# Transposing x on VectorE and through DRAM instead of on TensorE, in a linear attention with a gated MLP behind it

## The chip, the cores and the metric

One NeuronCore of one Trainium2 chip runs the whole program in one launch. The metric is the device time of an execution in microseconds; of the kernel before there are three runs, and their median counts. The engines' names are those of the profile: PE (TensorE matmuls; PEld is its weight loads), DVE (VectorE), ACT (ScalarE), POOL (GpSimd) and SP (SyncE, which here only issues DMAs).

## The reference

Attention with a feature map, for 4 batches of 4 heads, 1088 tokens and 32 dimensions, followed by a gated MLP with an RMS norm; the 4 x 1088 tokens are 4352 rows of 128:

```
phi(x)  = outer(S1 x, S2 x), 8 x 8 = 64 features per token and head
kv, z   = sum over tokens of phi(k) v, phi(k)
x       = phi(q) kv / (phi(q) z + 1e-6)           # 128 = 4 heads x 32 per token
xn      = x / sqrt(mean(x^2) + 1e-6) * rms_g
out     = (silu(xn @ w_gate) * (xn @ w_val)) @ w_out   # 128 -> 1536 -> 128
```

All inputs are float32; the MLP's weights and S1, S2 reach the chip as 64-bit words and are turned into float32 there.

## The kernel before, in words

**Tiling.** The tokens go in nine chunks, eight of 512 and one of 256. The 1536 hidden units go in 12 blocks of 128 (`j`). A *slot* is one chunk with one block: gate, value and down product (`slot`, L707). Each product is three matmul passes over 512 columns, since every operand is split into a high and a low fp32r part (`w_hi`, `w_lo`, `x_hi`, `x_lo`, `h_hi`, `h_lo`): lines 726 and 764. ACT takes the silu (L735), DVE multiplies (L738), ACT and DVE or POOL split the result (L753, L756).

**Ahead of the slots.** `kside(b)` (L450) makes batch b's kv: a matmul of the keys with `sblk` (S1 and S2 as blocks, L485), outer products (L439), and the sum over tokens on PE (L497; 64 columns of the array at a time for batch 0, 32 for the others). `qside(c)` (L528) makes chunk c's x: features `phiq`, then per 128 tokens the numerators and denominators (`nmm`, L620 to 630: PE holds 64 tokens of phiq as weights, 66 columns of kv stream through, two such tiles stand side by side in the array), the division (L636), the mean of squares (L655), its power on POOL (L668), the scaling `xn` (L671 or L688), a PE transpose of each 128 x 128 piece against an identity (`turn`, L673 to 675), and the split of the result, read from PSUM, into `x_hi` (ACT, L678) and `x_lo` (DVE, L681). From the third chunk on, phiq itself is built from matmul results that are stored to DRAM (`far`, L584) and read back in two layouts (`at`, `bt`, L596 and L602).

**S and the weights.** S is loaded by a DMA of ACT's queue (L392); an ACT and five DVE instructions (L371 to 389) make `sblk` from it, without which no matmul but the warming ones (L337) can start. Each of the 12 weight pieces (384 KB, L412) becomes float32 by five instructions of 128 x 384 (`to_f32`, L341), kept whole in `w_f`.

**What sets the order.** Every instruction is a task of a planner (`Plan`). A table of numbers (`ORDER`, L48) gives the order of all tasks, and a string (`ON`, L86) the engine of those that may run on several. The planner's own costs only place warming matmuls into gaps. So every engine, and SP's queue, runs its list strictly in order. At most eight DMAs of SP are in flight; the ninth waits for the first.

Of the kernel before, what the change touches and what calls it, by code (L numbers as in the profile page):

```python
# [84 lines left out]
"""  # L85
# [9 lines left out]
DEN_ACT = 60  # L95
QHALVES = 1
ABROWS = 1
WRAW = 7
LO_POOL, SCALED_ACT, PUT_ACT, COPY_DVE, PHI_POOL, H_POOL = 600, 100, 0, 300, 400, 900
UNIT, GAP, SPARE = 226, 400, 300  # L100
COLD = 5500
# [767 lines left out]
```

## Time and profile before

| | |
|---|---|
| median of 3 runs | 258.64 us (258.35 to 259.91) |
| profiled execution, span from the first to the last instruction | 256.5 us |
| PE busy | 252.0 us, 98% |
| DVE, ACT, POOL busy | 168.6, 153.8, 90.6 us |
| PE's share of the chain that ended last | 95% |

The page gives the profiled execution by its span alone; the median of the runs is 2.1 us above it, which is what lies around the instructions. Starts are counted from the span's start. A matmul's own duration overlaps the next one's, so the pace of PE is read from the differences of starts. A row with x32 is 32 instructions that follow one another; a float32 matmul stands as two instructions, a float32 transpose as one.

### The profile page before, as it was taken

The page shows a single profiled execution, that of the slowest core. Times are in us where ns is not written, and L with a number is a line of the kernel's source. Part 1 is how long each engine was busy: PE and PEld are TensorE (multiplying, and loading weights), DVE is VectorE, ACT ScalarE, POOL GpSimd, SP SyncE. Part 2 cuts the span into 40 slices and gives each one's busy share as a digit, 9 for nine tenths or more (in the row PEclk, how much of TensorE's full clock was granted, in tenths as well). Part 3 has the DMA queues.
Part 4 walks back from the last instruction along what each step waited for, and adds up shares of the span by engine and source line. Part 5 has one row for each costly group of instructions (what it writes and reads, how often), then busy time and mean ns, then how long its engine had stood idle before and what let it go on. Part 6 is the DMA issues. An engine that isn't in the chain of part 4 may idle for free.

```text
span 256.5 us, 5598 instructions
## 1 busy us (share of the span) xinstructions
PE 252.0 (98%) x2116; PEld 204.0 (80%) x2116; DVE 168.6 (66%) x390; ACT 153.8 (60%) x339; POOL 90.6 (35%) x92
## 2 busy tenths in 40 slices
PE   7999999999999999999999999999999999999995
PEld 5888777788887787788887888888888887888895
DVE  2998999989866676646464666647644554635643
ACT  3789888647664744575555555455556655554572
POOL 3444222123755412583516503145223714132031
PEclk9999999999999999999999999999999999999999
DMA  7999886064015115061320120001000100100010
GB/s 236 380 382 279 251 236 208 0 158 130 1 59 149 65 47 139 0 185 43 92 75 3 42 78 15 0 1 43 0 0 0 41 4 0 41 0 3 0 42 20
DMA packets 13498, 22.13 MB, mean 86 GB/s; under 512 B 1952, under 2 KB 5024, under 8 KB 13472
## 3 DMA queue, kind: packets, MB, share of 16 engines
q1 hardware_dynamic: 13040, 21.52, 27.0%
q8 instruction: 16, 0.26, 0.4%
q10 hardware_dynamic: 432, 0.26, 0.3%
q14 instruction: 10, 0.08, 0.1%
HBM read 18.69 MB, written 3.08 MB: 85 GB/s over the span
## 4 chain that ended last, share of the span: by engine, by line
PE 95%; ACT 2%; DMA 1%; POOL 1%; DVE 0%; issue 0%
PE g_ps L726 28%; PE v_ps L726 28%; PE o_ps L764 28%; PE att L627 3%; PE att L497 2%; PE att L675 2%; DMA s_raw<-sw 1%; PE att L485 1%; PE att L578 1%; PE o_ps L497 1%; ACT phiq L309 0%; ACT w_tmp L362 0%; POOL at L439 0%; PE att L745 0%; PE g_ps L485 0%; PE g_ps L558 0%
## 5 line engine op out<-in xcount | busy, mean ns | idle before, releaser
L738 DVE TENSOR_TENSOR h<-v_ps,s 128x512 f32<-128x512 f32 (+2 forms) x110 | 69.9, 649 | 49.7 <-PE v_ps L726 25.7
L756 POOL TENSOR_TENSOR h_lo<-h,h_hi 128x512 fp32r<-128x512 f32 (+1 forms) x43 | 53.0, 1242 | 109.2 <-DVE h_lo L756 39.7
L735 ACT ACTIVATE s<-g_ps 128x512 f32<-128x512 f32 (+1 forms) x108 | 60.8, 574 | 39.8 <-PE g_ps L726 32.7
L753 ACT CAST h_hi<-h 128x512 fp32r<-128x512 f32 (+1 forms) x106 | 61.3, 599 | 38.6 <-DVE h L738 35.5
L756 DVE TENSOR_TENSOR h_lo<-h,h_hi 128x512 fp32r<-128x512 f32 (+1 forms) x63 | 40.8, 660 | 13.4 <-ACT h_hi L753 10.0
L726 PE MATMUL g_ps<-x_hi,w_hi 128*128 128x512 f32 (+1 forms) x110 | 42.5, 387 | 0.0
L726 PE MATMUL v_ps<-x_hi,w_hi 128*128 128x512 f32 (+1 forms) x110 | 42.3, 385 | 0.0
L726 PE MATMUL g_ps<-x_lo,w_hi 128*128 128x512 f32 (+1 forms) x110 | 41.6, 379 | 0.0
L726 PE MATMUL v_ps<-x_hi,w_lo 128*128 128x512 f32 (+1 forms) x110 | 41.6, 378 | 0.0
L726 PE MATMUL g_ps<-x_hi,w_lo 128*128 128x512 f32 (+1 forms) x110 | 41.5, 378 | 0.0
L726 PE MATMUL v_ps<-x_lo,w_hi 128*128 128x512 f32 (+1 forms) x110 | 41.5, 379 | 0.0
L764 PE MATMUL o_ps<-h_hi,w_hi 128*128 128x512 f32 (+1 forms) x106 | 41.3, 389 | 0.0
L764 PE MATMUL o_ps<-h_hi,w_lo 128*128 128x512 f32 (+1 forms) x106 | 40.7, 384 | 0.0
L764 PE MATMUL o_ps<-h_lo,w_hi 128*128 128x512 f32 (+1 forms) x106 | 40.6, 383 | 0.0
L726 PEld LDWEIGHTS g_ps<-x_hi,w_hi 128*128 128x128 f32 x110 | 20.7, 188 | 4.8 <-ACT s L735 0.2
L726 PEld LDWEIGHTS v_ps<-x_hi,w_hi 128*128 128x128 f32 x110 | 20.7, 188 | 4.6 <-DVE h L738 0.3
L726 PEld LDWEIGHTS g_ps<-x_lo,w_hi 128*128 128x128 f32 x110 | 20.7, 188 | 4.2
L726 PEld LDWEIGHTS v_ps<-x_lo,w_hi 128*128 128x128 f32 x110 | 20.6, 188 | 4.2
L726 PEld LDWEIGHTS v_ps<-x_hi,w_lo 128*128 128x128 f32 x110 | 20.7, 188 | 4.0
L726 PEld LDWEIGHTS g_ps<-x_hi,w_lo 128*128 128x128 f32 x110 | 20.7, 188 | 3.9
L764 PEld LDWEIGHTS o_ps<-h_lo,w_hi 128*128 128x128 f32 x106 | 19.9, 188 | 4.3
L764 PEld LDWEIGHTS o_ps<-h_hi,w_hi 128*128 128x128 f32 x106 | 19.9, 188 | 4.1
(97 smaller groups left out, 256.5 us busy)
## 6 DMA issues: line engine op xcount, KB each, us to landing
w_raw<-w SPq DMA_DIRECT2D x12, 384.0 KB
bt<-far SPq DMA_DIRECT2D x24, 128.0 KB
at<-far SPq DMA_DIRECT2D x12, 256.0 KB
outT<-o_sb SPq DMA_DIRECT2D x8, 256.0 KB
q<-qT SPq DMA_DIRECT2D x7, 256.0 KB
vt<-v SPq DMA_DIRECT2D x4, 272.0 KB
kt<-kT SPq DMA_DIRECT2D x4, 256.0 KB
vt<-v SPq DMA_DIRECT2D x3, 340.0 KB
```

What stands on the lines that cost most here:

```text
L485: nc.tensor.matmul(out=ab()[n0:rows.stop, (t - lo) * HALF:(t - lo + 1) * HALF], lhsT=kt()[:, s0:s0 + len(rows)], rhs=sblk, start=True, sto ...
L497: nc.tensor.matmul(out=kvv[r0:r0 + wide, h // 2, :], lhsT=phi()[:, t, h * F + f:h * F + f + wide], rhs=vt()[:, t, h, :], start=(t == 0 and ...
L578: nc.tensor.matmul(out=accs[p]()[a * D:(a + 1) * D, :m], lhsT=sab[rows, p].rearrange("p c o r -> p (c o r)"), rhs=q()[rows, a * m:(a + 1) ...
L627: nc.tensor.matmul(out=nv[n0:rows.stop, t, p, :], lhsT=phi()[:, p, l0:l0 + len(rows)], rhs=kvs[cut][:, p, :], start=True, stop=True,)
L675: nc.tensor.transpose(out=xt()[:, t * P:(t + 1) * P], in_=xn()[:, t, :], identity=ident)
L726: nc.tensor.matmul(out=acc()[:, cs], lhsT=wt[:, j, i3, :], rhs=x()[:, cs], start=(i == 0), stop=(i == 2))
L735: act(n, lambda: nc.scalar.activation(out=s()[:, :n], in_=gps()[:, :n], func=AF.Silu), cols(gps, whole[0]), [s])
L738: cs.stop - cs.start, lambda cs=cs: nc.vector.tensor_tensor(out=h()[:, cs], in0=vps()[:, cs], in1=s()[:, cs], op=ALU.mult),
L753: act(n, lambda: nc.scalar.copy(out=h_hi()[:, :n], in_=h()[:, :n]), hs, [h_hi], True)
L756: eng.tensor_tensor(out=h_lo()[:, :n], in0=h()[:, :n], in1=h_hi().bitcast(F32)[:, :n], op=ALU.subtract)
L764: nc.tensor.matmul(out=o_ps()[:, :n], lhsT=wt[:, j, 2, :], rhs=x()[:, :n], start=first and i == 0, stop=last and i == 2,)
```

## The change

From the third chunk on (`XT = 2`, `spread`), x is no longer transposed by PE. The scaled x is written into `xn` in the order head, tile, dimension; one DVE instruction transposes each 32 x 32 block of it (`xq`); four DMAs of SP, one per head, store the blocks to DRAM (`turned`) in rows of 128 tokens (512 B each), and one more loads the whole, now with the 128 features on the partitions, to `xt` in SBUF. ACT's and DVE's split into x_hi and x_lo reads `xt` there and not from PSUM. For that layout the numerators are taken with 32 tokens as weights and not 64: twice as many matmuls of the same 66 columns, four tiles side by side. S is loaded by SP's queue and no longer by ACT's. The whole float32 weights live in a rotating buffer (`w_full`, three of them), and only the last two blocks' output weights are copied to `w_f`. `ORDER` and `ON` are new throughout.

```diff
+XT = 2
...
-    plan.add({"dma": Way(
-        ISSUE + SLATE, P * NB * 8 / 320, lambda: nc.scalar.dma_start(out=s_raw.rearrange("p n c -> p (n c)"), in_=sw.bitcast(U32)), since=740
-    )}, (), ["s_raw"])
+    load(P * NB * 8, lambda: nc.sync.dma_start(out=s_raw.rearrange("p n c -> p (n c)"), in_=sw.bitcast(U32)), ["s_raw"])
...
-            def nmm(u=u, num=num):
+            wide = D if spread else HALF
+
+            def nmm(u=u, num=num, wide=wide):
                 nv = num()[:, :4 * 66].rearrange("p (t a x) -> p t a x", t=2, a=2)
                 for t in range(2):
                     for p in range(2):
-                        for rows in range(HALF), range(HALF, P):
-                            l0, n0 = (u + t) * P + rows.start, rows.start
-                            cut = (s0 + l0) // S
+                        for n0 in range(0, P, wide):
+                            l0 = n0 // D * g + (u + t) * D if spread else (u + t) * P + n0
                             nc.tensor.matmul(
-                                out=nv[n0:rows.stop, t, p, :], lhsT=phi()[:, p, l0:l0 + len(rows)], rhs=kvs[cut][:, p, :],
-                                start=True, stop=True,
+                                out=nv[n0:n0 + wide, t, p, :], lhsT=phi()[:, p, l0:l0 + wide], rhs=kvs[(s0 + l0) // S][:, p, :], start=True, stop=True,
                             )
...
+            if spread:
+                xq, xt = sb("xq", [P, 4 * DM], 1), sb("xt", [P, 512], 1)
+                dve(n, lambda: nc.vector.transpose(out=xq()[:, :n], in_=xn()[:, :n]), [(xn, u)], [xq], True)
+                turned = plan.buf(dram, [DM, 512], F32, "turned", 2)
+
+                for h in range(H):
+                    def put_far(h=h, turned=turned, xq=xq):
+                        nc.sync.dma_start(
+                            out=turned()[h * D:(h + 1) * D, :n].rearrange("d (a s) -> a d s", a=4), in_=xq()[:, h * g:(h + 1) * g]
+                        )
+
+                    plan.add({"dma": Way(ISSUE, 200, put_far)}, [xq], [(turned, h)])
+                load(P * n * 4, lambda: nc.sync.dma_start(out=xt()[:, :n], in_=turned()[:, :n]), [xt], [(turned, h) for h in range(H)])
+                got = [xt]
+            else:
+                xt = ps("att", ATT)
...
```

Two places of the new order. First PE around the third chunk's numerators; `phiq` is the weights, `kv` streams. Before:

```order
L726 MATMUL g_ps_1012<-x_hi_571,w_hi 128x512
L726 MATMUL g_ps_1012<-x_hi_571,w_lo 128x512
L726 MATMUL g_ps_1012<-x_lo_589,w_hi 128x512
L627 MATMUL att_1021<-kv_75,phiq_892 64x66 x8
L627 MATMUL att_1036<-kv_73,phiq_892 64x66
L627 MATMUL att_1036<-kv_75,phiq_892 64x66
```

And now:

```order
L761 MATMUL g_ps_911<-x_hi_439,w_hi 128x512
L761 MATMUL g_ps_911<-x_hi_439,w_lo 128x512
L761 MATMUL g_ps_911<-x_lo_460,w_hi 128x512
L638 MATMUL att_921<-kv_75,phiq_879 32x66 x16
L638 MATMUL att_941<-kv_73,phiq_879 32x66
L638 MATMUL att_941<-kv_75,phiq_879 32x66 x3
```

The matmuls are twice as many and half as wide, and they stand earlier, ahead of gate matmuls that still read the first chunk's x. The group `L675 MATMUL att_1259<-ident,xn_1232 128x128 x4` that followed later on PE has no successor.

Second the start of the program on DVE, where `sblk` is made from `s_raw`. Before:

```order
L371 TENSOR_SCALAR s_top<-s_raw 128x64
L382 TENSOR_SCALAR s_tmp<-s_tmp 128x64
L374 SCALAR_TENSOR_TENSOR s_top<-s_raw,s_top 128x64
L386 TENSOR_SCALAR s_tmp<-s_tmp 128x64
L389 TENSOR_TENSOR sblk<-s_tmp,s_top 128x64
L310 COPY both_143<-att_127 128x128
L439 TENSOR_TENSOR at_152<-att_127,both_143 128x512
```

And now:

```order
L346 TENSOR_SCALAR w_tmp_114<-w_raw_100 128x384
L374 TENSOR_SCALAR s_top<-s_raw 128x64
L385 TENSOR_SCALAR s_tmp<-s_raw 128x64
L388 TENSOR_SCALAR s_tmp<-s_tmp 128x64
L352 TENSOR_SCALAR w_tmp_114<-w_tmp_114 128x384
L377 SCALAR_TENSOR_TENSOR s_top<-s_raw,s_top 128x64
L392 TENSOR_SCALAR s_tmp<-s_tmp 128x64
L356 TENSOR_SCALAR w_tmp_114<-w_tmp_114 128x384
L395 TENSOR_TENSOR sblk<-s_tmp,s_top 128x64
L360 SCALAR_TENSOR_TENSOR w_tmp_114<-w_raw_100,w_tmp_114 128x384
L363 SCALAR_TENSOR_TENSOR w_full_145<-w_raw_100,w_tmp_114 128x384
```

The first weight piece's five instructions now stand among those that make `sblk`, and on SP's queue its 384 KB DMA stands first and S's second:

```order
L414 DMA w_raw_100<-w 128x768
L397 DMA s_raw<-sw 128x128
L462 DMA kt_106<-kT 128x512
L529 DMA q_102<-qT 128x256
L462 DMA kt_106<-kT 128x641
```

Before, SP's list began with the three last of these kinds, keys, queries, keys, and S was ACT's.

## Rows read from the trace of the kernel before

**Rows 1.** The page, its head and part 1: busy time, share, instructions.
```profile
span 256.5 us, 5598 instructions
...
PE 252.0 (98%) x2116; PEld 204.0 (80%) x2116; DVE 168.6 (66%) x390; ACT 153.8 (60%) x339; POOL 90.6 (35%) x92
```

**Rows 2.** The page's chain of waits, by engine.
```profile
PE 95%; ACT 2%; DMA 1%; POOL 1%; DVE 0%; issue 0%
```

**Rows 3.** Windows: stretch, busy us of each engine, PEclk, DMA share, GB/s.
```profile
22.21:235.81 213.60, 213.60 (x1621) 170.87 (x1618) 141.25 (x306) 127.95 (x263) 78.41 (x69) 1.00 0.23 68
```

**Rows 4.** PE's timeline around one group of transposes: start, us, engine, line, tiles.
```profile
70.34 0.39 PE L726 MATMUL v_ps<-x_hi,w_lo 128*128 128x512 f32 x1
70.57 0.39 PE L726 MATMUL v_ps<-x_lo,w_hi 128*128 128x512 f32 x1
70.81 0.60 PE L675 MATMUL att<-ident,xn 128*128 128x128 f32 x4
...
71.48 0.39 PE L764 MATMUL o_ps<-h_hi,w_lo 128*128 128x512 f32 x1
```

**Rows 5.** PE's timeline: numerators of one chunk, and of one and a half.
```profile
53.54 1.16 PE L627 MATMUL att<-kv,phiq 128*64 128x66 f32 x32
54.63 0.50 PE L726 MATMUL g_ps<-x_hi,w_hi 128*128 128x512 f32 x1
...
163.85 1.62 PE L627 MATMUL att<-kv,phiq 128*64 128x66 f32 x48
165.40 0.50 PE L726 MATMUL v_ps<-x_hi,w_hi 128*128 128x512 f32 x1
```

**Rows 6.** PE's timeline: a batch's kv, 32 columns of the array each.
```profile
50.26 0.40 PE L726 MATMUL v_ps<-x_lo,w_hi 128*128 128x512 f32 x1
50.59 1.44 PE L497 MATMUL att<-vt,phi 128*32 128x34 f32 x144
51.95 0.50 PE L764 MATMUL o_ps<-h_hi,w_hi 128*128 128x512 f32 x1
52.29 0.39 PE L764 MATMUL o_ps<-h_hi,w_lo 128*128 128x512 f32 x1
```

**Rows 7.** PE's timeline: query matmuls alone, and with a batch's kv behind them.
```profile
26.71 0.40 PE L726 MATMUL g_ps<-x_lo,w_hi 128*128 128x512 f32 x1
...
27.75 0.39 PE L726 MATMUL g_ps<-x_hi,w_lo 128*128 128x512 f32 x1
...
86.23 0.40 PE L764 MATMUL o_ps<-h_lo,w_hi 128*128 128x512 f32 x1
...
88.64 0.39 PE L726 MATMUL g_ps<-x_hi,w_lo 128*128 128x512 f32 x1
```

**Rows 8.** The timeline of the start, all engines; in brackets idle time before.
```profile
0.73 0.41 ACTq L392 DMA_DIRECT2D s_raw<-sw  x1
...
4.01 0.20 DVE L371 TENSOR_SCALAR s_top<-s_raw 128x64 uint32<-128x64 uint32 x1 [3.14 <-DMA s_raw<-sw]
...
5.04 0.34 PE L485 MATMUL g_ps<-sblk,kt 128*64 128x64 f32 x4 [0.70 <-DVE sblk L389]
...
5.99 0.69 DVE L439 TENSOR_TENSOR at<-att,both 128x512 f32<-128x512 f32 x1
6.31 1.07 POOL L439 TENSOR_TENSOR at<-both 128x512 f32<-128x512 f32 x1
...
7.43 0.66 PE L558 MATMUL g_ps<-ident,at 128*128 128x128 f32 x4
```

**Rows 9.** DVE's timeline: instructions that turn a weight piece into float32.
```profile
20.75 0.35 DVE L350 TENSOR_SCALAR w_tmp<-w_tmp 128x384 uint32<-128x384 uint32 x1
21.02 0.35 DVE L346 TENSOR_SCALAR w_tmp<-w_tmp 128x384 f32<-128x384 f32 x1
21.29 0.55 DVE L354 SCALAR_TENSOR_TENSOR w_tmp<-w_raw,w_tmp 128x384 uint32<-128x384 uint32 x1
```

**Rows 10.** SP's timeline: a store to DRAM in four DMAs, and the load behind it.
```profile
146.58 1.74 SPq L584 DMA_DIRECT2D far<-abt  x4
149.54 0.56 SPq L596 DMA_DIRECT2D at<-far  x1
```

**Rows 11.** The page, part 5: DVE from SBUF to SBUF, 128x512.
```profile
L756 DVE TENSOR_TENSOR h_lo<-h,h_hi 128x512 fp32r<-128x512 f32 (+1 forms) x63 | 40.8, 660 | 13.4 <-ACT h_hi L753 10.0
```

More of the change, by code (lines that the diff above doesn't have):

```diff
@@ L101 @@
 COLD = 5500
-SWITCH = 98
+SWITCH = 138
 RING, ISSUE, FAR, FLIGHT, SETTLE = 8, 470, 640, 1650, 250
@@ L329, in attention_then_glu @@
     sab = const.tile([P, 2, 2, 2, R], F32, name="sab")
-    w_f = const.tile([P, NJ, 3, P], F32, name="w_f")
+    w_f = const.tile([P, LAST_EXACT, P], F32, name="w_f")
     w_hi = const.tile([P, NJ, 3, P], F32R, name="w_hi")
@@ L343, in a, with a_act @@
             nc.vector.tensor_scalar(out=tmp().bitcast(U32), in0=raw()[:, :, 1], scalar1=0x7FFFFFFF, scalar2=None, op0=ALU.bitwise_and)
+        def a_act():
+            nc.scalar.activation(out=tmp(), in_=raw()[:, :, 1].bitcast(F32), func=AF.Abs)
         def b():
@@ L359, in f @@
             )
-        def a_act():
-            nc.scalar.activation(out=tmp(), in_=raw()[:, :, 1].bitcast(F32), func=AF.Abs)
         plan.add({"act": on_act(n, a_act, True), "dve": on_dve(n, a, fast=True, against=100)}, reads, tt)
@@ L379, in s_abs, with s_abs_dve @@
         nc.scalar.activation(out=s_tmp, in_=s_raw[:, :, 1].bitcast(F32), func=AF.Abs)
+    def s_abs_dve():
+        nc.vector.tensor_scalar(out=s_tmp.bitcast(U32), in0=s_raw[:, :, 1], scalar1=0x7FFFFFFF, scalar2=None, op0=ALU.bitwise_and)
     def s_clamp():
@@ L409, in weights @@
     def weights(j):
+        plan.family = f"weights{j}"
         raw, tmp = sb("w_raw", [P, 3 * P, 2], WRAW, U32), sb("w_tmp", [P, 3 * P], 3)
@@ L415, in weights, with rest @@
         )
-        to_f32(3 * P, lambda: w_f[:, j].rearrange("p a n -> p (a n)"), raw, tmp, [raw], [tmp], [("w_f", j)])
+        full = sb("w_full", [P, 3, P], 3)
+        to_f32(3 * P, lambda: full().rearrange("p a n -> p (a n)"), raw, tmp, [raw], [tmp], [full])
+        if j >= NJ - LAST_EXACT:
+            act(P, lambda: nc.scalar.copy(out=w_f[:, j - NJ + LAST_EXACT], in_=full()[:, 2]), [full], [("w_f", j)], True)
         for part, lo, hi in ((0, 0, 2), (1, 2, 3)):
             n = (hi - lo) * P
-            f, h, l = (x[:, j, lo:hi] for x in (w_f, w_hi, w_lo))
-            act(n, lambda f=f, h=h: nc.scalar.copy(out=h, in_=f), [("w_f", j)], [("w_hi", j, part)], True)
-            def rest(eng, f=f, h=h, l=l):
-                eng.tensor_tensor(out=l, in0=f, in1=h.bitcast(F32), op=ALU.subtract)
+            h, l = (x[:, j, lo:hi] for x in (w_hi, w_lo))
+            act(n, lambda lo=lo, hi=hi, h=h: nc.scalar.copy(out=h, in_=full()[:, lo:hi]), [full], [("w_hi", j, part)], True)
+            def rest(eng, lo=lo, hi=hi, h=h, l=l):
+                eng.tensor_tensor(out=l, in0=full()[:, lo:hi], in1=h.bitcast(F32), op=ALU.subtract)
             plan.add(
                 {"dve": on_dve(n, lambda rest=rest: rest(nc.vector), True), "pool": on_pool(n, lambda rest=rest: rest(nc.gpsimd), LO_POOL)},
-                [("w_f", j), ("w_hi", j, part)], [("w_lo", j, part)],
+                [full, ("w_hi", j, part)], [("w_lo", j, part)],
             )
@@ L450, in kside @@
     def kside(b):
-        plan.family = "keys"
+        plan.family = f"keys{b}"
         first = b == 0
@@ L528, in qside @@
     def qside(c):
-        plan.family = "queries"
+        plan.family = f"queries{c}"
         n, s0 = CHUNKS[c], STARTS[c]
@@ L612, in qside @@
                 }, [(at, p), (bt, p, 0), (bt, p, 1)], [(phi, "p", p)])
-        x, xn = sb("x", [P, 4, DM], 2), sb("xn", [P, 4, DM], 1)
+        spread = c >= XT
+        g = n // 4
+        x, xn = sb("x", [P, 4, H, D], 2), sb("xn", [P, 4 * DM], 2)
         ms, rstd = sb("ms", [P, 4], 2), sb("rstd", [P, 4, 1], 2)
@@ L654, in mean @@
                 def mean(t=t, u=u, sq=sq):
+                    one = x()[:, u + t]
                     nc.vector.tensor_tensor_reduce(
-                        out=sq(), in0=x()[:, u + t], in1=x()[:, u + t], scale=1.0 / DM, scalar=EPS, op0=ALU.mult, op1=ALU.add,
+                        out=sq().rearrange("p (h d) -> p h d", h=H), in0=one, in1=one, scale=1.0 / DM, scalar=EPS, op0=ALU.mult, op1=ALU.add,
                         accum_out=ms()[:, u + t:u + t + 1],
@@ L668, in root, with scaled @@
                 nc.gpsimd.tensor_tensor(out=rstd()[:, us, 0], in0=ms()[:, us], in1=mhalf[:, us], op=ALU.pow)
-            def scaled(us=us, wd=wd):
-                nc.vector.tensor_tensor(out=xn()[:, us], in0=x()[:, us], in1=rstd()[:, us].to_broadcast([P, wd, DM]), op=ALU.mult)
-            def turn(u=u, wd=wd, xt=xt):
-                for t in range(u, u + wd):
-                    nc.tensor.transpose(out=xt()[:, t * P:(t + 1) * P], in_=xn()[:, t, :], identity=ident)
+            def scaled(u=u, wd=wd):
+                nc.vector.tensor_tensor(
+                    out=scaled_of(u, u + wd), in0=x()[:, u:u + wd],
+                    in1=rstd()[:, u:u + wd].unsqueeze(3).to_broadcast([P, wd, H, D]), op=ALU.mult,
+                )
@@ new lines, in scaled_act @@
+            def scaled_act(u=u, wd=wd):
+                for t in range(u, u + wd):
+                    nc.scalar.activation(out=scaled_of(t, t + 1)[:, 0], in_=x()[:, t], func=AF.Copy, scale=rstd()[:, t])
+            plan.add({"pool": Way(400 + 150 * wd, 430 + 150 * wd, root)}, [(ms, i) for i in range(u, u + wd)], [(rstd, u)])
+            plan.add({
+                "dve": on_dve(wd * P, scaled, True),
+                "act": Way(wd * 300 + 5, wd * 300 + 85, scaled_act, against=SCALED_ACT),
+            }, [(x, i) for i in ids] + [(rstd, u)], [(xn, u)])
@@ new lines, in qside, with turn @@
+            if spread:
+                xq, xt = sb("xq", [P, 4 * DM], 1), sb("xt", [P, 512], 1)
[5 more added lines that the diff above has]
+                            out=turned()[h * D:(h + 1) * D, :n].rearrange("d (a s) -> a d s", a=4), in_=xq()[:, h * g:(h + 1) * g]
+                        )
+                    plan.add({"dma": Way(ISSUE, 200, put_far)}, [xq], [(turned, h)])
+                load(P * n * 4, lambda: nc.sync.dma_start(out=xt()[:, :n], in_=turned()[:, :n]), [xt], [(turned, h) for h in range(H)])
+                got = [xt]
+            else:
+                xt = ps("att", ATT)
+                def turn(u=u, wd=wd, xt=xt):
+                    for t in range(u, u + wd):
+                        nc.tensor.transpose(out=xt()[:, t * P:(t + 1) * P], in_=xn()[:, t * DM:(t + 1) * DM], identity=ident)
+                pe(wd * 108, turn, [(xn, u)], [xt], tiled=0)
+                got = [xt]
@@ L677, in high, with low @@
             def high(cs=cs, xt=xt):
                 nc.scalar.activation(out=x_hi()[:, cs], in_=xt()[:, cs], func=AF.Copy, scale=gain_t)
-            def low(cs=cs, xt=xt):
-                nc.vector.scalar_tensor_tensor(
+            def low(eng, cs=cs, xt=xt):
+                eng.scalar_tensor_tensor(
                     out=x_lo()[:, cs], in0=xt()[:, cs], scalar=gain_t, in1=x_hi().bitcast(F32)[:, cs], op0=ALU.mult, op1=ALU.subtract
                 )
-            plan.add({"pool": Way(400 + 150 * wd, 430 + 150 * wd, root)}, [(ms, i) for i in range(u, u + wd)], [(rstd, u)])
@@ L686, in scaled_act @@
-            def scaled_act(u=u, wd=wd):
-                for t in range(u, u + wd):
-                    nc.scalar.activation(out=xn()[:, t], in_=x()[:, t], func=AF.Copy, scale=rstd()[:, t])
-            plan.add({
-                "dve": on_dve(wd * P, scaled, True),
-                "act": Way(wd * 205 + 20, wd * 205 + 120, scaled_act, against=SCALED_ACT),
-            }, [(x, i) for i in ids] + [(rstd, u)], [(xn, u)])
-            pe(wd * 108, turn, [(xn, u)], [xt], tiled=0)
-            plan.add({"act": Way(wd * 107 + 155, wd * 107 + 255, high)}, [xt, "gain"], [(x_hi, u)])
@@ L696, in qside @@
-            dve(wd * P * 1.12, low, [xt, "gain", (x_hi, u)], [(x_lo, u)])
+            plan.add({"act": Way(wd * 107 + 155, wd * 107 + 255, high)}, [*got, "gain"], [(x_hi, u)])
+            dve(wd * P * 1.12, lambda low=low: low(nc.vector), [*got, "gain", (x_hi, u)], [(x_lo, u)], spread)
     runs = [(c, range(*r)) for r in ((0, CUT), (CUT, NJ)) for c in range(2)] + [(c, range(NJ)) for c in range(2, len(CHUNKS) - 1)]
@@ L745, in slot @@
                     (cs.stop - cs.start) * 1.676 + 4, lambda cs=cs, o=o: nc.tensor.matmul(
-                        out=o()[:, cs], lhsT=w_f[:, j, 2], rhs=h()[:, cs], start=first, stop=last
+                        out=o()[:, cs], lhsT=w_f[:, j - NJ + LAST_EXACT], rhs=h()[:, cs], start=first, stop=last
                     ),
```

22 lines of the change are left out of this document (11 added, 11 removed), and 74 rows, old and new, of the table ORDER.

## The prediction

> **What bounds the kernel now.** I read the page's head first: PE is busy 252.0 of 256.5 us, 83 us more than DVE [rows 1]. A busy share alone would not decide it, since PE's durations overlap; so the chain of waits came next, and 95% of the span on it is PE's own work, with next to nothing for DMA [rows 2]. The windows then show where PE is without a gap: from 22.21 to 235.81 us it is busy in 213.60 of 213.60 us [rows 3]. In that stretch whatever is taken from PE's list shortens the run by as much, and what is added to another engine costs nothing until PE waits for it. At the start it is otherwise: PE's first real matmul at 5.04 us waits for `sblk`, and every list is strict behind it [rows 8]: what delays the first matmul delays the end.
>
> **Transposes removed.** Around a group of four, PE's starts go from 70.57 to 71.48 us; without it two passes at the pace of 0.23 us (70.34 to 70.57) would stand there: 0.91 - 0.46 = 0.45 us, or 0.11 for each [rows 4]. The chunks from the third on have six such groups and one of two, 26 transposes: 26 x 0.11 = **-2.9 us**, all of it in the stretch without a gap.
>
> **Numerators.** With 64 tokens as weights, 32 instructions take 1.09 us and 48 take 1.55 [rows 5]; the difference gives 0.46 / 16 = 0.029 us each, 0.92 for a chunk, and 0.17 that comes once for an excursion from the full array. Two tiles run side by side, so one instruction takes 0.058. With 32 tokens there are 64 instructions, four side by side. What each takes no row shows. From below: a float32 transpose streams 128 columns in 0.11 us [rows 4], so 66 columns take at least 0.056, and 64 / 4 x 0.056 = 0.90. From above, four tiles that gain nothing over two: 64 x 0.029 = 1.84. The nearest row is the batches' kv, also 32 columns wide with four tiles in turn: 144 instructions in 1.36 us, 0.009 each, so the four do run side by side [rows 6]. I take 0.90, **-0.1 us** over the 6.5 chunks.
>
> **Excursions.** Each change from the full array to narrow tiles and back costs PE something. Query matmuls alone add 1.04 - 0.46 = 0.58 us, a batch's kv alone 2.03 - 0.46 = 1.57 [rows 6, 7], and both in one go 2.41 - 0.46 = 1.95 [rows 7]: merging two saves 0.20. By the order there are 13 such excursions between gate matmuls before and 11 now: **-0.4 us**.
>
> **The start.** Here the change loses. S is not first on SP's queue: the 384 KB weight piece is. Before, S was issued on ACT's queue at 0.73 us and usable at 4.01, and PE started 1.03 us behind that [rows 8]. Now S is issued one DMA later on SP; an issue takes 0.4 us, as ACT's did [rows 8]. Its wait may partly vanish in the 3.28 us that it takes anyway. Between the instructions that make `sblk` DVE now has two of 128x384; such ones follow each other at 0.27 us [rows 9], so 0.54 for both. One step (the absolute value) moves from ACT to DVE, and ACT's queue is free of S's issue, which gains nothing, because ACT then waits. Together I take +0.6; the bounds are +0.1, if the DVE instructions fill waits that the dependent steps have anyway and S lands as before, and +1.0, if all of it adds.
>
> Behind `sblk` the queries' outer products `at` are late next. Before, DVE and POOL shared them and PE transposed them at 7.43 us, 2.39 behind its first matmul [rows 8]. Now both are DVE's, 0.69 each, behind two 128x384 instructions of 0.55 [rows 8, 9] and a small product of a first key tile: about 2 x 0.55 + 0.5 + 2 x 0.69 = 3.0 us behind `sblk`, and PE has only key and query matmuls to fill that. The wait grows by some 0.5 us; it could be 0 if later stalls shrink by as much, since the weights' work done here is DVE's gain later, or 1.0. The start is **+1.1 us**, between +0.1 and +2.0.
>
> **Work that lies beside PE.** VectorE's block transpose has no row. The nearest is DVE from SBUF to SBUF at the same size, 0.66 us [rows 11]; half of that below and double above are the bounds. The four stores cost SP 1.74 us of issuing, as the `far` stores do, which have the same 512 B rows; a load waiting for them was issued 2.96 us after the first [rows 10]. The load's own way is at most the 3.28 us of S at the start [rows 8], and two loads of `at` and `bt` stand ahead of it on SP for the third chunk, 0.56 each [rows 10]. From `xn` to `xt` that is 0.66 + 2.96 + 1.1 + 3.3 = 8.0 us where PE needed 0.45. What covers it is the earlier numerators: by the order, 26 groups of three passes stood between the third chunk's numerators and the first gate matmul that reads its x, and 36 stand there now; for the next chunk 26 and 35, for the later ones 52 or more. Ten groups at 0.70 us (three passes) are 7.0 us. So the third and fourth chunk just get by, the others easily: **0 us**, at worst 1 to 2 us for each of the two. The reads from SBUF in place of PSUM, the two small copies into `w_f`, and the scaling into strided rows are ACT's and DVE's, which have 88 us and more to spare [rows 1].
>
> On the stores the Trainium skill ("VectorE: DVE Perf Modes", section on the three transpose paths) speaks against the change: a plain DMA that transposes by strides is many times slower than a proper one where the destination's innermost stride is large. The `far` stores do not bear it out, four in 2.96 us with all waiting, since within 512 B the rows are contiguous; by the rule the x of every chunk would be late.
>
> **Sum.** -2.9 - 0.1 - 0.4 + 1.1 = -2.3 us: the profiled execution's 256.5 us span becomes 254.2, and with the 2.1 us between span and median 258.64 becomes **256.3**. That is -0.9%, and about 1%, 2.6 us, is what a measurement of this kernel tells from no change; so 256.05 us separates "faster" from "same".
>
> **Rivals.**
> *The start costs nothing.* The extra DVE work falls into waits between dependent steps, and S lands no later. For it: DVE idled 3.14 us ahead of S [rows 8]. Against: the two long instructions stand between the steps, not ahead. Then -3.4 + 0.1: 255.3 us.
> *The start costs all of its bounds*, +2.0 and a little more behind it: 257.5 us. For it: every engine's list is strict there.
> *x comes late.* The third and fourth chunk's load lands after PE needs it, 1 to 2 us each, or all seven by a little: 258.5 us, up to 261.5. For it: the chain of 8.0 us against 7.0 gained. Against: of the 26 groups before, not all were needed.
> *The narrow numerators do not run side by side* (the other side). If each instruction has a floor of its own as in the 64-wide form, 0.029 us, a chunk costs 1.84 and not 0.90: +0.94 x 6.5 = +6.1, 262.4 us, 1.5% slower. It decides from 0.014 + 2.3 / 416 = 0.020 us per instruction on: there the gain is gone. Against: 0.009 for the kv matmuls [rows 6].
> The Trainium skill ("TensorEngine Tiling (Array Packing)", section on instruction overhead) has such a floor, about 60 cycles a matmul; at 2.4 GHz 0.025 us, by which, if tiles didn't overlap it, I estimate 260.9. The kv rows' 0.009 us contradict that for tiles in turn.
>
> **Chances.** The forecast 0.47, of which 0.17 fall below 256.05; the costless start 0.25; the costly start 0.07; late x 0.16, a quarter of it slower than 261.2; no side-by-side 0.05. Faster by over 1%: 0.17 + 0.25 = 0.42. Slower by over 1%: 0.05 + 0.04 = 0.09. Same: 0.49. The range reaches from 254.8, a start without loss and numerators at their lower end, to 258.8, half of the late cases; outside are the floor, the other half and a little below: under 0.2.
>
> **What would show it.** No L675-like transposes from the third chunk on, and PE's starts around their former place at 0.23 us. Numerators: 64 instructions in about 1.07 us with the fixed part; 1.9 would mean the floor. The first keys' matmul at about 5.6 us, and the queries' transposes at about 8.5. PE without a gap behind 25 us; a gap ahead of a first gate matmul of a chunk, released by x_hi or x_lo, would be late x. I am wrong if PE's saving is below 3 us, or if the start loses outside 0.1 to 2.0.

## The result and the profile after

| | before | after |
|---|---|---|
| median of the runs side by side | 259.22 us | 261.79 us |
| span of the profiled execution | 256.5 us | 259.1 us (its time 261.21) |

The ratio is 1.011 (95% interval 1.008 to 1.014): the change made the kernel **slower by 1.1%**. Forecast were 256.3 us and a range to 258.8, so the prediction was wrong. The ratios further down leave out three disturbed executions (265.4 us in e1, 408.8 in e5, 490.5 in e7), and since those of e1 and e5 are their profiled ones, neither profile is argued from alone. The head of the page, PE's share and the chain, after (answering to [rows 1, 2]):

```profile
span 259.1 us, 6070 instructions
PE 249.9 (96%) x2308; PEld 202.6 (78%) x2308; DVE 177.2 (68%) x405; ACT 153.3 (59%) x345; POOL 82.7 (32%) x85
PE 90%; DVE 4%; issue 2%; DMA 1%; POOL 1%; ACT 1%
```

PE has 2.1 us less to do and needs 2.6 us more. The chain has an entry that had 0% before: "issue", time in which an engine waits for nothing that the profile shows. The waits of PE in the kernel after, by line (waited for, us, times, longest):

```profile
PE att L502 <- issue: 1.8, 1, 1.8
PE att L638 <- issue: 1.5, 1, 1.5
PE v_ps L490 <- DVE sblk L395: 0.9, 1, 0.9
...
PE g_ps L761 <- issue: 0.6, 1, 0.6
PE g_ps L761 <- ACT x_hi L723: 0.3, 1, 0.3
```

Three waits for "issue", 3.84 us together (PE's timeline gives them as 1.79, 1.47 and 0.58). The same stretch of the windows as in [rows 3] has PE busy in 210.34 of 213.60 us:

```profile
22.21:235.81 213.60, 210.34 (x1824) 169.08 (x1825) 147.97 (x314) 128.98 (x273) 67.13 (x59) 1.00 0.29 87
```

The 3.26 us that are missing are the two longer waits. PE's timeline shows where they stand:

```profile
71.82 0.40 PE L799 MATMUL o_ps<-h_lo,w_hi 128*128 128x512 f32 x1
72.15 1.14 PE L638 MATMUL att<-kv,phiq 128*32 128x66 f32 x64
73.10 1.53 PE L502 MATMUL att<-vt,phi 128*32 128x34 f32 x106
76.43 0.54 PE L502 MATMUL att<-vt,phi 128*32 128x34 f32 x38 [1.79 <-issue]
...
118.46 0.62 PE L502 MATMUL att<-vt,phi 128*32 128x34 f32 x47
...
120.66 0.57 PE L638 MATMUL att<-kv,phiq 128*32 128x66 f32 x25 [1.47 <-issue]
```

Each lies in the middle of a run of one instruction group on the same operands: the 107th kv matmul of one batch reads the same tiles as the 106th, and the profile has nothing that released it. That speaks against a late operand. Both stand in the places where the new order has put numerators and a batch's kv into one dense excursion.

**Accounting**, by PE's starts. The first 512-column matmul: 22.21 us before, 24.34 after (+2.13, of which 1.25 is the first matmul that reads x, 17.60 to 18.85, and 0.58 the third wait; the other 0.30 is not traced further). That matmul is a gate or a value matmul, by the order; below it is called the first gate matmul. From the first 512-column matmul to PE's last start: 231.30 before, 231.46 after (+0.16). Behind it: 2.99 and 3.30 (+0.3). Sum +2.6, the difference of the spans. So the saving on PE is there (3.1 to 3.2 us) and the two gaps have eaten it; the start then makes the loss.

### The profile page after: what moved, and what is told of

It is laid out like the page before. It is cut to its first block, busy times and chain, and to the rows that moved or that the text cites. A ratio compares the mean times of both kernels' runs of the same rounds, so it can differ in the third digit from the quotient of the medians.

```text
span 259.1 us, 6070 instructions
## 1 busy us (share of the span) xinstructions
PE 249.9 (96%) x2308; PEld 202.6 (78%) x2308; DVE 177.2 (68%) x405; ACT 153.3 (59%) x345; POOL 82.7 (32%) x85
## 4 chain that ended last, share of the span: by engine, by line
PE 90%; DVE 4%; issue 2%; DMA 1%; POOL 1%; ACT 1%
PE g_ps L761 28%; PE v_ps L761 28%; PE o_ps L799 27%; PE att L638 3%; PE att L502 2%; DMA w_raw<-w 1%; PE att L583 1%; PE att L490 1%; POOL phi L444 1%; DVE w_tmp L360 0%; DVE w_full L363 0%; POOL rstd L681 0%; DVE phi L444 0%; DVE at L444 0%; DVE w_tmp L356 0%
## 5 line engine op out<-in xcount | busy, mean ns | idle before, releaser
L770 ACT ACTIVATE s<-g_ps 128x512 f32<-128x512 f32 (+1 forms) x108 | 61.5, 574 | 50.2 <-PE g_ps L761 32.1
L791 POOL TENSOR_TENSOR h_lo<-h,h_hi 128x512 fp32r<-128x512 f32 (+1 forms) x44 | 54.2, 1244 | 99.9 <-ACT h_hi L788 28.1
```

Of the source, the lines that this page charges most:

```text
L770: act(n, lambda: nc.scalar.activation(out=s()[:, :n], in_=gps()[:, :n], func=AF.Silu), cols(gps, whole[0]), [s])
L791: eng.tensor_tensor(out=h_lo()[:, :n], in0=h()[:, :n], in1=h_hi().bitcast(F32)[:, :n], op=ALU.subtract)
```

## What PE waits for

The trace also holds the DMAs by which an engine's instructions are loaded (queue 8). The kernel after has 18 of them, before 16, each of 16,384 bytes. I numbered PE's instructions (a float32 matmul stands as four there, two weight loads and two matmuls; the semaphore waits and drains that the trace lists on PE count too; 4658 in all after and 4266 before) and set the loads beside the gaps:

```
                     gap behind    border      load of the       PE goes
                     instruction   before at   instructions      on at
after, 21.28 us          705        14.92     19.84 to  20.76     22.14
after, 74.44 us         1985        72.76     73.83 to  75.10     76.43
after, 118.97 us        3009       117.20    118.08 to 119.40    120.66
```

705, 1985 and 3009 all leave 193 when divided by 256, and PE goes on 1.26 to 1.38 us after a load has landed. **Theory 1**: PE's instructions come in blocks of 256; the load of the next block starts about 1 us after PE has passed a border, takes about 1 us and is usable 1.3 to 1.4 us later, some 3.5 to 3.7 us in all for the two later gaps. 256 instructions of wide matmuls last 29 us. The two blocks of narrow ones above are used up in 1.7 us (72.76 to 74.44, 117.20 to 118.97), and PE runs dry. The early gap at 21.28 us is of another kind: its block lasts 6.4 us, but the load began 4.9 us after the border. Whether a dense group holds a whole block depends on where the borders fall. **Theory 2**: x's stores and loads, new in the change, crowd out something PE needs. **Theory 3**: a hidden wait (a buffer, a semaphore) of the new order.

## The experiments

Every ratio is to the kernel before, run side by side; the two columns of times are of the profiled execution. "Stretch" is from PE's first 512-column start to its last start; [rows 3] lie in it.

| run | ratio (95%) | first gate matmul | stretch, us |
|---|---|---|---|
| before | | 17.60 | 231.30 |
| after | 1.011 (1.008 to 1.014) | 18.85 | 231.46 |
| e1 before, list +224 | 1.010 (1.006 to 1.013) | 20.48 | 235.42 |
| e8 before, list +144 | 1.022 (1.017 to 1.027) | 18.90 | 235.46 |
| e2 after, list +256 | 1.029 (1.023 to 1.036) | 20.83 | 233.26 |
| e5 after, list +160 | 0.998 (0.995 to 1.001) | | |
| e6 after, S first | 1.020 (1.013 to 1.027) | 19.61 | 231.38 |
| e7 e5's list, e6's start | 1.000 (0.997 to 1.003) | 19.44 | 228.07 |
| e4 after, piece late | 1.023 (1.017 to 1.029) | 22.73 | 232.22 |
| e9 groups apart | 1.004 (1.002 to 1.006) | 18.96 | 230.65 |
| e11 the same, mended | 1.001 (0.998 to 1.003) | 18.94 | 228.95 |
| e10 e9 and a start | 1.018 (1.013 to 1.022) | 21.75 | 230.89 |
| e12 e11 and e6's start | 0.998 (0.996 to 1.000) | 19.21 | 228.61 |

**e1 and e2: the same list, shifted.** Small matmuls ahead of the first wait, nothing else:

```diff
-WARM = 8
+WARM = 4
...
     keep_warm(WARM)
+    tiny = psum.tile([P, 512], F32, name="att0", bufs=1)
+    for _ in range(60):                                   # e2: 68
+        nc.tensor.matmul(out=tiny[:1, :1], lhsT=zeros[:, :1], rhs=zeros[:, :1], start=True, stop=True)
```

> The kernel before, with PE's instruction list lengthened by 112 in front: four of the eight warming matmuls are replaced by 60 of one column (two instructions each), all ahead of the first wait for sblk. Nothing else changes, no DMA, no order. Theory 1 (PE's instructions arrive in blocks of 256, one load a block, and a block that PE uses up faster than about 3.7 us leaves PE dry until the next has arrived; where the blocks' borders fall in the narrow matmuls decides): with the borders moved by 112, three excursions into narrow matmuls of this kernel now fill a block each, near 52, 91 and 130 us, and PE stands still there 2.2, 2.1 and 2.4 us, released by nothing the profile shows; the time rises by 4.5 to 7 us, to 264 to 266. Theory 2 (the gaps of the changed kernel come from the stores and loads of x that now go through DRAM) and theory 3 (they come from a wait or a buffer in the changed order): this kernel has neither, so no gap and 258.5 to 260, at most 0.6 us at the start for the small matmuls.

> The changed kernel, with PE's instruction list lengthened by 128 in front, by 68 matmuls of one column in place of four warming ones. Order, DMAs and buffers are the same. Theory 1: the borders of the blocks now fall beside the dense groups of narrow matmuls, the gaps of 1.79 us (at 74.6) and 1.47 us (at 119.2) go or shrink below 0.5 us each, and the time falls by 2.5 to 3.8 us to 258 to 259.3, unless the small matmuls push the start back (up to 0.6 us). Theories 2 and 3: both gaps stay at their places with their lengths, 261 to 262.5.

I had counted two instructions to a float32 matmul. It is four, so e1 moved the borders by 224 and e2 by 256, a whole block. As it was forecast, e2 spoke for theories 2 and 3; with the count put right it is a control: its gaps stay at the same matmuls (2.04 and 1.68 us, behind instructions 2241 and 3265, again 193 over a multiple of 256). That correction came after the result, so the tests are e5, e7 and e8, which were forecast with it. e1 is the kernel *before*, without x's DMAs and with its own order, and it now has a gap, at 90.8 us, where the shifted border falls (PE's timeline, e1):

```profile
89.45 0.45 PE L581 MATMUL att<-q,sab 64*32 64x128 f32 x16
89.83 1.12 PE L500 MATMUL att<-vt,phi 128*32 128x34 f32 x106
93.42 0.76 PE L500 MATMUL att<-vt,phi 128*32 128x34 f32 x38 [2.47 <-issue]
```

Again behind number 2241. Theories 2 and 3 can't make this one (e8 below repeats it). The times themselves were missed: e1 has one gap for the three forecast, since with the shift of 224 only one block, of 2.79 us, falls into narrow matmuls, and e2 lost 2 us at the start to the small matmuls.

**e3: narrow matmuls alone**, behind the end of the kernel before, no data moving:

```diff
+    for i in range(768):
+        n0 = i % 4 * 32
+        nc.tensor.matmul(out=bench[n0:n0 + 32, :66], lhsT=zeros[:, :32], rhs=zeros[:, :66], start=True, stop=True)
+    for i in range(512):
+        n0 = i % 2 * 64
...
```

> The kernel before, and behind its last matmul, where no load runs any more: 48 matmuls of 384 columns, 768 matmuls of 32 weights columns and 66 columns streamed (four side by side), 512 of 64 weight columns (two side by side), 24 of 384 columns; their results are used by nothing. Theory 1: the narrow matmuls run in bursts of 128 (256 instructions) and a gap follows each, so that 128 take about 3.7 us from one gap's end to the next instead of 128 x 16 ns = 2.1 us; the 768 take about 22 us and not 12.3; one instruction load of 16 KB belongs to each burst; the 384 columns wide ones show no gap. Theories 2 and 3: no gaps, since no DMA of data runs beside them and nothing is waited for; 768 x 16 ns = 12.3 us.

```profile
267.94 2.12 PE L818 MATMUL att<-const-float32-0.0 128*32 128x66 f32 x128 [1.01 <-issue]
271.67 2.12 PE L818 MATMUL att<-const-float32-0.0 128*32 128x66 f32 x128 [1.61 <-issue]
275.12 2.12 PE L818 MATMUL att<-const-float32-0.0 128*32 128x66 f32 x128 [1.33 <-issue]
278.58 2.12 PE L818 MATMUL att<-const-float32-0.0 128*32 128x66 f32 x128 [1.33 <-issue]
...
309.50 28.18 PE L821 MATMUL att<-const-float32-0.0 128*64 128x66 f32 x931 [0.26 <-issue]
```

Ten bursts of exactly 128 matmul instructions (256 with the weight loads) from 267.94 to 305.50 us: **3.76 us a block**, one 16 KB load in each, each gap behind number 193. That is theory 1 by itself. (768 matmuls are 1536 such instructions, so they took 43 us and not the 22 I wrote: the same counting error.) At 64 columns a block lasts 3.84 us from border to border and the gaps are gone: that pace just fits.

**e5, e7, e8: the borders set on purpose**, with the count mended.

```diff
-WARM = 8
+WARM = 4                       # e7: 3, e8: 4 in the kernel before
+    for _ in range(44):        # e7: 50, e8: 40; one column, as in e1
```

> The changed kernel with PE's list lengthened by 160 instructions in front. A float32 matmul stands in that list as four instructions, not two, so the run before this one had moved the borders by a whole block of 256, and its gaps stayed at the same places, each behind instruction 193 of a block of 256 as in every other run. Now 44 matmuls of one column take the place of four of the eight warming ones, 40 more in all; order, DMAs and buffers are as in the changed kernel. Theory 1 (blocks of 256 PE instructions, each there about 3.7 us after the border before it; the 193rd counted from the first record is the border): no block lies within the dense narrow groups any more, the gaps of 0.9, 2.0 and 1.7 us (differences of starts at 21.3, 74.4 and 119.0) fall below 0.4 each, and the time to 257 to 258.6. Theory 2 (stores and loads of x) and theory 3 (a wait or buffer in the changed order): gaps as before, 261 to 262.5.

> The changed kernel with both edits: the start with S first, and PE's list lengthened by the 160 instructions that put the borders of its blocks outside the dense groups. If theory 1 and the start theory hold and add up: 256 to 257.5, no gap over 0.4 us behind 20 us, the first gate matmul near 17.8; this would be the prediction's own sum without a loss at the start (255.3 to 256.3) plus what little is left of gaps. If the gaps had another cause: 260 to 261.2.

> The kernel before with PE's list lengthened by 144 instructions (40 matmuls of one column for four warming ones), which puts three borders into its narrow groups; nothing else changes. Theory 1: three gaps, each behind the 193rd instruction of a block of 256, near 52, 91 and 130 us, of 2.0 to 2.6 us each, and a time of 264.5 to 268, since the granted clock fell for some us behind a gap of 2.7 us in the run with this kernel shifted by 224. Theories 2 and 3: this kernel has neither the stores of x nor the changed order, so no gap and 258.3 to 259.

e8 has its three gaps where they were forecast, behind 1473, 2241 and 3009, shorter (1.1 to 1.8 us between starts, for 2.0 to 2.6): two of the three loads began within 0.2 us of the border and not 1 us behind it, which theory 1 does not explain. The stretch is 4.2 us longer than before's; another 1.3 us of e8's loss stands at the start, with its small matmuls. PE's timeline in e8, two of them:

```profile
51.91 1.30 PE L500 MATMUL att<-vt,phi 128*32 128x34 f32 x128
54.47 0.33 PE L500 MATMUL att<-vt,phi 128*32 128x34 f32 x16 [1.26 <-issue]
...
93.20 0.39 PE L729 MATMUL g_ps<-x_lo,w_hi 128*128 128x512 f32 x1 [1.38 <-issue]
```

e5 is the changed kernel with nothing but warming matmuls replaced, and its borders moved by that: the ratio of 1.011 has become 0.998 (0.995 to 1.001), some 3.4 us less, and the kernel can't be told from the one before. The gaps are read from e7, whose list has the same length. Windows, e7, the same 213.60 us from the first 512-column matmul on:

```profile
24.01:237.61 213.60, 213.56 (x1831) 172.27 (x1824) 149.82 (x318) 132.29 (x277) 69.48 (x61) 1.00 0.28 83
```

No gap, with all of x's stores and loads in place; the stretch is 228.07 us, **3.2 us less than before's**, what the prediction had credited to PE (3.4). e7's own forecast of the time (256 to 257.5 us) was missed all the same: its median is 258.5, and the first gate matmul comes at 19.44, not near 17.8.

**e9 and e11: the groups taken apart**, borders where they are in the kernel after. The PE tasks of `ORDER` at the two places (463, 470, 424, 431, 440, 447, 693, 701, 714, 617 are wide):

```diff
-... 463 470 424 431 518 512 298 302 306 440 447 ...
+... 424 431 518 512 463 470 440 447 298 302 306 ...        # e11; e9 leaves 463 470 ahead
-... 693 993 485 489 760 493 766 701 617 714 715 ...
+... 993 485 489 693 701 714 617 760 493 766 715 ...
```

> The changed kernel with PE's list of the same length and its block borders where they were, but the two dense groups taken apart in the order: near 72 us the numerators are moved ahead of two down products and two more stand between them and the kv matmuls (12 wide matmuls between 64 and 144 narrow instructions); near 116 us four wide tasks (12 matmuls) stand in the middle of the group. No small matmuls are added. Theory 1: each block of 256 instructions now lasts over 4 us, so the gaps behind the 193rd instruction at 74.4 and 119.0 fall below 0.3 us; two excursions more cost 0.2 us each; the gap near 21.3 stays; 257.6 to 259. Theories 2 and 3: x's stores and loads are the same, and a wait on a buffer would move with the matmul that waits: a gap of 1.5 to 2 us stays somewhere in these groups, 261 to 262.5.

> The changed kernel, its start and PE's list length as they are, with the two dense groups taken apart again, now so that the wide matmuls between are ready and nobody queues behind a late one: near 72 us two value tasks and two down products stand between the numerators and the kv matmuls; near 116 us four tasks stand in the middle of the group, and ScalarE's two copies of denominators from the late half stand behind the silu and the split of those tasks. In the run before, no gap was left at a block's border there, but 1.2 and 1.8 us of waits for VectorE behind those copies had come in their place. Theory 1: no gap at either place, 257.4 to 259; what is left over the prediction's sum is the start and the gap near 21.3. Theories 2 and 3: 1.5 to 2 us of gap stay in these groups, 260 to 262.

In e9 both late gaps at a border are gone (the early one stays), and two others have come, with a releaser and at no border: 0.78 us for VectorE's `o_sb` at 74.89, and this one:

```profile
123.09 0.50 PE L761 MATMUL v_ps<-x_hi,w_hi 128*128 128x512 f32 x1 [1.55 <-DVE h L773]
```

ScalarE's list held the denominators of the moved numerators ahead of the silu that VectorE, and with it PE, needed. With that mended (e11) one wait of 0.58 us is left there, for ScalarE's silu at 78.10, and the stretch is 228.95. Its profile has 1.71 us of the early gap (number 705), 0.58 in the kernel after; its runs reach from 257.5 to 260.6 us, which I put down to this gap without having shown it.

**The start: e4, e6, e10, e12.** In the kernel after (answering to [rows 8]):

```profile
0.74 0.40 SPq L414 DMA_DIRECT2D w_raw<-w  x1
1.20 0.41 SPq L397 DMA_DIRECT2D s_raw<-sw  x1
...
4.54 0.36 DVE L346 TENSOR_SCALAR w_tmp<-w_raw 128x384 uint32<-128x384 uint32 x1 [3.67 <-DMA w_raw<-w]
4.90 0.20 DVE L374 TENSOR_SCALAR s_top<-s_raw 128x64 uint32<-128x64 uint32 x1
...
6.39 0.57 PE L490 MATMUL v_ps<-sblk,kt 128*64 128x64 f32 x12 [0.94 <-DVE sblk L395]
...
8.73 0.63 PE L563 MATMUL g_ps<-ident,at 128*128 128x128 f32 x4
...
18.85 0.38 PE L761 MATMUL g_ps<-x_hi,w_hi 128*128 128x256 f32 x1 [0.31 <-ACT x_hi L723]
```

VectorE's first instruction waits for the weight piece until 4.54 us, and S, which stands behind it on VectorE's list, waits with it; before, VectorE had S at 4.01. I had not put this wait in. Edits of SyncE's and VectorE's lists were to bring that back (the warming matmuls change with them, so that PE's list keeps its length):

```
SyncE:   -w S kt q kt q vt ...      e6, e12: +S w kt q kt ...     e4: +S kt q kt q vt w ...     e10: +S kt w q ...
VectorE: -w S S S w S S w S w w ...   e6, e12: +S S S S S S w w w copy product at at w w ...
```

> The changed kernel with its start in the old order: on SyncE's queue S stands first, then keys, queries and values, and the first weight piece seventh; on VectorE the six instructions of sblk stand first and the piece's five stand behind the first products; five warming matmuls become five of one column, so that PE's list keeps its length and the borders of the instruction blocks stay. Start theory: what delays the first matmul to 6.39 us is the piece ahead of S on the queue and its instructions among those of sblk; undone, the first matmul starts at 5.0 to 5.3, PE's transposes at 7.4 to 7.8, and 0.8 to 1.3 us of the time come back, 260.4 to 261.1, with both late gaps still there. Rival: S suffers from SyncE's queue itself, where its 64 KB share the engines with the other loads: first matmul not before 6.0, no change of the time (261.3 to 262.3). Second rival: the piece that comes later delays the first gate matmul and the start gains nothing: first matmul early, but the time unchanged.

> The changed kernel with S ahead of the first weight piece on SyncE's queue (these two change places, no other DMA moves), the six instructions of sblk first on VectorE, the piece's five behind them (three ahead of the first products, two behind), and its two ACT and two POOL splits behind the next copy and product there. The length of PE's list is kept, so the borders of its blocks stay. Start theory: the first matmul starts at 4.7 to 5.2 instead of 6.39, PE's transposes at 7.5 to 8.2 instead of 8.73, the first gate matmul 0.7 to 1.3 us earlier than 18.85, and the time falls by as much to 260.2 to 261.2; the gaps near 73.5 and 118 stay. Rival: the first gate matmul is held by the weights or the mean of squares behind it, stays at 18.5 to 19, and the time at 261.3 to 262.4.

> The same, and a start with S first, the first keys second and the weight piece third on SyncE's queue; on VectorE S's six instructions first, the piece's spread behind the first copies, one of its five on ScalarE; PE still has 8 wide warming matmuls ahead of the real ones (5 of one column ahead of them keep the list's length, since a run with mostly small ones left the first real matmuls at half their pace). Start theory: first matmul at 4.6 to 5.2, PE's transposes at 7.3 to 8.2, first gate matmul at 17.7 to 18.4 (18.85 in the changed kernel), and 0.4 to 1.2 us less than the kernel with the groups split alone: 256.5 to 258.2, faster than before by a little. Rival: VectorE has the same work to do until 18 us and no more time in which it is ready, so the first gate matmul stays at 18.6 to 19 and the time with that of the split alone (within 0.4 us).

> The same, with the start of the run that had S ahead of the weight piece (S first, then the piece, then keys; S's instructions first on VectorE), and all 13 warming matmuls wide and ahead of the first real one, so that no small matmuls or idle time stand ahead of it. Start theory: the keys land near 5.6 us behind the piece, the first matmul starts at 5.7 to 6.2 at full pace, PE's transposes at 7.8 to 8.4, the first gate matmul at 18.0 to 18.6; 0.3 to 0.8 us less than the kernel with the groups taken apart alone: 256.8 to 258.4. Rival: the first gate matmul at 18.7 to 19.2 as VectorE's list decides it, no gain.

S first works as far as S goes: it lands at 3.0 us and `sblk` is there at 4.0 (e4). But then the keys are late (5.7 us in e6), or the queries (e10), or the weights: in e4 PE stood for 2.3 us at 18.03, since ScalarE's list has the splits of the late piece ahead of `phiq`. In none does the first gate matmul start before 19.2. In e12 the first matmul starts 0.5 us earlier than in the kernel after, the transposes at 8.19 for 8.73, and the gate matmul at 19.21:

```profile
5.87 0.57 PE L490 MATMUL v_ps<-sblk,kt 128*64 128x64 f32 x12 [0.16 <-DVE w_tmp L352]
...
19.21 0.38 PE L761 MATMUL g_ps<-x_hi,w_hi 128*128 128x256 f32 x1 [0.31 <-ACT x_hi L723]
```

The rival was right: `sblk` alone does not set that matmul. e12 has no gap without a releaser anywhere (also not the early one) and, with e5, the lowest ratio, but with 0.998 (0.996 to 1.000) it can't be told from the kernel before.

**e13 to e15: the whole old start**, some 100 tasks in the order and on the engines of the kernel before, S on ScalarE's queue, with the groups apart (e13, e15) and without (e14):

```diff
-    load(P * NB * 8, lambda: nc.sync.dma_start(out=s_raw...), ["s_raw"])
+    plan.add({"dma": Way(..., lambda: nc.scalar.dma_start(out=s_raw...), since=740)}, (), ["s_raw"])
```

> The changed kernel with the two dense groups taken apart as in the mended run, and with the whole start of the kernel before up to the first gate matmul: its order and its engines on PE, VectorE, ScalarE, GpSimd and SyncE (some 100 tasks), and S on ScalarE's queue again; 8 wide warming matmuls, 5 of one column ahead of them to keep the list's length. Start theory A (the loss of 1.25 us at the first gate matmul lies in what the start's new order gives VectorE, not in sblk alone, which came at 4.0 us in the run before and helped nothing): the first gate matmul starts at 17.5 to 18.1 as in the kernel before, no gap at a border near 21, 74 or 119, and 255.6 to 256.8 in all, 0.6 to 1.1% faster than before; this is then the prediction's sum without its loss at the start. Theory B (the loss comes from elsewhere, such as the float32 weights' rotating buffer): the first gate matmul stays near 18.9, 257.2 to 258.5.

> The changed kernel with the start of the kernel before alone, its dense groups left whole and the list's length kept. Theory 1 with A: the gaps near 73.2 and 117.8 stay with 1.4 to 2.1 us each, the first gate matmul at 17.5 to 18.1, 259.2 to 260.8, between the changed kernel and the run with the groups apart. With B: 260.4 to 262.4.

> The run with the old start and the groups apart once more, with ScalarE's and VectorE's lists in the order of the kernel before up to the second split of x (there, some weight splits stood ahead of the scaling of x and held PE for 1.9 us at 18.6). Start theory A (the loss at the first gate matmul lies in the start's new order and engines): first gate matmul at 17.5 to 18.3, the time 255.6 to 257.2. Theory B (elsewhere, such as the rotating float32 weights): 18.7 or later, 257.2 or more.

All three were slower (1.011, 1.025 and 1.013) and say nothing on theory A or B: at the seam of the two orders ScalarE held PE up (1.95 us ahead of 18.62 in e13), and the first gate matmul came at 20.3 to 21.9. What they do show again is theory 1: e14, with the groups whole, has gaps of 1.9 and 1.7 us (between starts) behind 1985 and 3009; e13 and e15 have 0.45 us and nothing there.

## Why the prediction was wrong

**The step that failed** is "in that stretch whatever is taken from PE's list shortens the run by as much", with its test "PE without a gap behind 25 us". I took a PE that is busy in 213.60 of 213.60 us [rows 3] for a PE that is limited by its matmuls alone. It has a supply of instructions as well. In the kernel before the borders fall so that no block behind 20 us lasts less than 6.1 us (one of them cuts the kv group of [rows 6] in two, at 51.20); e8, which moves the borders by 144 instructions, adds 4.2 us to that kernel's stretch. In the kernel after two borders fall so that a whole block lies in narrow matmuls; 1.79 and 1.47 us are lost there, 0.58 at the start.

The Trainium skill has this supply ("Runtime: NRT & Kernel Launch", section on instruction fetch mechanics): blocks of 16 KiB, 256 instructions, the next one loaded while the current one runs, and the load hidden because instructions are issued more slowly than they arrive. The loads and the blocks agree with this trace; that they are hidden does not, at 1.7 us for a block that takes 3.7 to arrive. I had not weighed it.

Point by point:
- **Excursions, -0.4.** The saving was near: without gaps the stretch is 228.07 us with the two groups merged (e7) and 228.61 with them apart (e12). What it left out is worth more. Merging is what made the runs dense: at 72 us numerators (64 matmul instructions) and kv (144) now follow each other, at 116 us queries, kv and numerators (16, 144 and 64). In the kernel after, taking them apart (e11) shortens the stretch by 2.5 us.
- **Transposes, -2.9, and numerators, -0.1.** Right as far as shown: with the excursions they were to give 3.4, and without gaps the stretch is 3.2 us shorter (e7); no run has the transposes alone. The 64 numerators of a chunk take 1.06 us against 1.07 forecast (46.12 to 47.18):

```profile
46.12 1.13 PE L638 MATMUL att<-kv,phiq 128*32 128x66 f32 x64
47.18 0.50 PE L761 MATMUL g_ps<-x_hi,w_hi 128*128 128x512 f32 x1
```

  So four narrow tiles do run side by side, and the rival with a floor is out.
- **The start, +1.1.** The size was near (first gate matmul +1.25 us; transposes 8.73 for "about 8.5"), but by luck. The first matmul came at 6.39 for "about 5.6", 1.35 us later than before and outside the bound of 1.0, of which 0.53 is VectorE's wait for the weight piece, which was missing from the sum, and 0.83 the longer way to `sblk` (4.54 to its instruction at 6.12, before 4.01 to 4.76); and the wait of 2.39 us behind it, which was to grow by 0.5, stayed at 2.34. Nor was the reason shown: e6 and e12 take away the wait for `sblk` and gain nothing at the gate matmul. What delays that one stays open; ahead of it VectorE is busy 11.68 us up to 16.4 us, before 10.89. With the early gap the first 512-column matmul came 2.13 us later, a little more than the upper bound.
- **x through DRAM, 0.** Right: a transpose on VectorE takes 0.70 us, and the only wait was ScalarE's 0.40 for the third chunk's `xt`, which didn't reach PE (nor does PE wait for x in e7, where no gap gives x time). The strided-copy trap of the Trainium skill ("VectorE: DVE Perf Modes", section on the three transpose paths), weighed there, did not show.

```profile
65.09 0.70 DVE L700 STREAM_TRANSPOSE xq<-xn 128x512 f32<-128x512 f32 x1
73.97 0.72 ACT L723 ACTIVATE x_hi<-xt,gain_t 128x512 fp32r<-128x512 f32 x1 [0.40 <-DMA xt<-turned]
```

- None of my rivals was what happened. With the gaps put in the sum closes: 256.5 - 3.2 + 1.25 + 3.84 + 0.3 = 258.7, of 259.1 in the profiled execution. And without the gaps the change gains nothing that can be told (0.998 to 1.000 in e5, e7 and e12): of the 3.2 us that e7 saves in the stretch, 1.8 go to its later first 512-column matmul and 0.3 to its end.

## What to carry to other kernels

A saturated PE had a second limit here, its supply of instructions: count the instructions of every run of short ones, and where 256 of them last clearly less than about 3.7 us (e7 has blocks of 3.64 and 3.67 us without a gap), put wide work between or expect a gap with "issue" as its releaser. Such a gap sits at a fixed count of instructions, so any edit ahead of it, even a few warming matmuls, moves it, and a small gain or loss measured on such a kernel may be alignment and not the edit: here 1.3% between two kernels that differ in 44 small matmuls for four warming ones. To test it, shift the list and leave the work alone.

## What was not expected of the hardware

- PE resumed 1.26 to 1.53 us after a block's load had landed, in 17 gaps of three kernels (after, e3, e8). The load itself took 0.9 to 1.4 us. It began 0.8 to 1.6 us after the border with no data moving (e3), but 4.9 us after it in the kernel after at 14.92 us, while the inputs were being loaded, and within 0.2 us of it in two gaps of e8.
- Behind the gap of 2.04 us in e2 the granted clock fell, to 0.69 of full in the mean of the 4 us that hold the gap's end; passes then came 0.43 us apart instead of 0.23, as at the lower of the two levels (1.2 and 2.4 GHz). Behind 1.79 us (after) it did not. The length of a gap alone does not settle it: behind the wait of 2.1 us in e4 (PE goes on at 124.47) it stayed at 1.00, and behind one of 1.9 us in e14 (on at 18.77) it was 0.50 from 20 to 24 us. Windows of e2:

```profile
72.00:76.00 4.00, 3.75 (x176) 3.00 (x175) 2.77 (x4) 1.01 (x3) 0.00 (x0) 1.00 0.58 191
76.00:80.00 4.00, 2.21 (x42) 1.85 (x42) 1.87 (x3) 2.26 (x6) 1.27 (x1) 0.69 0.71 181
```

- In some runs the first real matmuls ran at a lower pace, though the windows give the clock as 1.00: 12 instructions took 0.91 us in e6 (12 wide warming instructions from 0.77 us on, then 14 of one column) and in e10 (10 of one column, then 16 wide ones from 1.22 us on), and 0.57 in the kernel after (24 wide ones from 0.78 us on) and in e4 (16 wide ones from 0.78 us on, then 10 of one column). What decides it stays open.
